# Attention block: the products with v in two groups of five pairs per unit, and TensorE's attention work in strict source order

## The chip, the cores and the metric

The kernel runs on one core of a Trainium2 chip. A core has a TensorE for matrix products (PE; PEld is its weight load), a VectorE (DVE), a ScalarE (ACT), a GpSimd (POOL) and a SyncE that issues DMAs (SP). The metric is the device time of one execution in microseconds (us). The kernel before takes 1155.64 us, the median of three runs from 1153.95 to 1157.52.

## What is computed

Attention with a learned position bias, over 4 batches, 8 heads, 576 positions and 64 dimensions a head, followed by two feed-forward layers on 2304 tokens of 512 features. All is float32.

```python
scores = scale * np.matmul(q, k.transpose(0, 1, 3, 2)) + bias      # bias: a small network of the positions
scores = scores - np.max(scores, axis=-1, keepdims=True)
attn = np.exp(scores)
attn = attn / (np.sum(attn, axis=-1, keepdims=True) + 1e-09)
x = np.matmul(attn, v)                                             # -> 2304 x 512
h = x @ w_in;  x = (h * np.clip(h + 3.0, 0.0, 6.0) / 6.0) @ w_out
out = (1 / (1 + np.exp(-(x @ w_gate))) * (x @ w_val)) @ w_out2
```

## The kernel before

The program has four stages: the position bias (to about 57 us of the profile), attention (to about 337 us), and the two feed-forward layers. The change touches attention alone.

Attention works in 16 units, each two heads of one batch, and each unit in nine steps. Steps 0 to 7 take 128 queries of one head, the two heads in turn; step 8 takes the last 64 queries of both heads. A step t goes through these functions:

- `scores` (line 365): four matmuls of 128x288, ten of them in step 8, into a PSUM tile "s" (two buffers, two banks each). Then VectorE adds the bias into an SBUF tile "u" and keeps the row's minimum (line 378).
- `expo` (line 392): ScalarE's exponential into the tile "p" or "pm", with the row's sum.
- `trans` (line 426): four transposes of 128x128 on TensorE into a PSUM tile "tr" (three buffers, one bank each), which VectorE or ScalarE copies out to the tile "ptm" (`evac`, the letters of `PT_EVAC`).
- `trans_rem` (line 440): after steps 1, 3, 5 and 8, one transpose (two after step 8) for the last 64 keys of both heads, into another "tr" tile and from there to the tile "ptr", on ScalarE.
- `invert` (line 397) and `turn_inv` (line 407): twice a unit, after steps 5 and 8, VectorE inverts the sums, ScalarE spreads them, and three or two transposes into a "tr" tile turn them; copies of VectorE and ScalarE bring them to the tile "inv".
- `av` (line 450): the products with v, in two groups a unit, one for each half of the queries (a = 0, 1), into the PSUM tile "av" (one buffer). A group has five pairs (g = 0 to 4), each pair one product for each head, written to the two halves of the partitions; the first four read ptm, the last reads ptr. A float32 product shows as two matmul records, so a pair shows as four. `av_out` (line 464) multiplies by inv on VectorE into the input of the next layer.

`slot_of_two` (line 490) takes two steps at a time. Slot i traces, in this order: the scores of steps 2i and 2i+1, the products that `AV` holds for the slot, the two exponentials, `invert` for the steps of the slot before, `turn_inv` for the steps of two slots before, `trans` and `trans_rem` for the steps of the slot before, and a cast of the next unit's queries and keys. Some slots also carry a piece of preparing the first layer's weights, on ScalarE, VectorE and GpSimd. `AV` (lines 479 to 485) puts three pairs of a group in one slot and two in the next, so that eight slots in nine hold products.

A planner (the framework's scheduler) puts the instructions into each engine's queue. It takes the source order as a priority, and lets an instruction pass an earlier one of the same engine where it reckons the earlier one is not ready. Each engine then executes its queue in order. `tc.issue_after(x)` binds everything traced inside it, on the engine of x, to come behind x in that queue; it adds no wait. The kernel before binds the transposes of a slot behind the last score matmul traced (line 516) and nothing else of TensorE.

Of the kernel before, what the change touches and what calls it, by code (L numbers as in the profile page):

```python
# [1 line left out]

# [1 line left out]

# [14 lines left out]
P = 128  # L19
B, H, S, D = 4, 8, 576, 64  # L20
# [4 lines left out]
HS = S // 2  # L25
# [71 lines left out]
def block_kernel(ctx: ExitStack, tc: tile.TileContext, q, k, v, mlp, w_in, w_out, w_gate, w_val, w_out2, dist_d,  # L97
                 rows_d, out):
    nc = tc.nc
# [199 lines left out]
    Pm = [apool.tile([P, S], F32, name=f"pm{i}") for i in range(2)]  # L299
    ident = apool.tile([P, P], F32, name="ident")  # L300
    stat = apool.tile([P, 5, NSTEP, 2], F32, name="stat")
    low, sums = [stat[:, i, :, 0] for i in range(2)], [stat[:, i, :, 0] for i in range(2, 5)]
    spread = apool.tile([P, 5 * P], F32, name="spread")
# [10 lines left out]
    def load_v(n):  # L314
        vn[n] = a2.tile([P, 10, D], F32, name="vn")
        return nc.sync.dma_start(vn[n], v[n])

    def load_bias(p, c):
        n = min(P, S - P * c)
        rows_of = nbias[c][15 : 15 + n * (8 * RK - 1)].rearrange("(i q) -> i q", i=n)  # L320
        for h in range(2):
            o = bias_t[c][:, h] if c < 4 else bias_m[64 * h : 64 * h + 64]
            i = rows_of[:, RK * (2 * p + h) : RK * (2 * p + h) + S]
            if c == 4 and h == 1:
                nc.sync.dma_start(o[:, 0:512], i[:, 64:S])
                nc.sync.dma_start(o[:, 512:S], i[:, 0:64])
            else:
                nc.sync.dma_start(o, i)
# [23 lines left out]
    NS = NU * NSTEP  # L352
    ptm = apool.tile([P, 2, 4, S], F32, name="ptm")
    ptr = apool.tile([P, S], F32, name="ptr")
    pts, us, avs, last_u, last_s = {}, {}, {}, [None], [None]

    seq = [(n, s) for n in range(NU) for s in range(NSTEP)]

    def keys(s, h, a):

        if s < 8 or h == 0:
            return [(HS * a, 0, HS)]
        return [(64, 0, HS)] if a == 0 else [(64 + HS, 0, HS - 64), (0, HS - 64, 64)]

    def scores(t):
        n, s = seq[t]
        Q, K = Qs[n % 2], Ks[n % 2]
        ps = pp.tile([P, 2, 512], F32, name="s")
        todo = [(s % 2, s // 2)] if s < 8 else [(0, 4), (1, 4)]
        for a in range(2):  # L370
            mm = [(h, c, r, part) for h, c in todo for r in range(2) for part in keys(s, h, a)]
            for i, (h, c, r, (k0, o, w)) in enumerate(mm):
                q0 = (0, S + P)[h] + P * c if c < 4 else (512, S)[h]
                last_s[0] = nc.tensor.matmul(ps[:, a, o : o + w], Q[:, q0 : q0 + P], K[:, r, h, k0 : k0 + w],  # L374
                                             start=(i == 0), stop=(i == len(mm) - 1))
        u = a2.tile([P, S], F32, name="u", bufs=3)
        bt = bias_t[s // 2][:, s % 2] if s < 8 else bias_m
        last_u[0] = nc.vector.tensor_tensor_reduce(  # L378
            out=halves(u), in0=ps[:, :, 0:HS], in1=halves(bt), op0=ALU.add, op1=ALU.min, scale=-0.125, scalar=3e38,
            accum_out=low[n % 2][:, s : s + 1])  # L380
        us[t] = u
# [25 lines left out]
    def turn_inv(n, c0, c1):  # L407

        ps = pp.tile([P, 4, P], F32, name="tr", bufs=3)
        for c in range(c0, c1):  # L410
            nc.tensor.transpose(ps[:, c % 3], spread[:, P * c : P * c + P], ident)  # L411
        if c1 == 3:
            evac("A", inv[:, 0 : 3 * P].rearrange("p (c q) -> p c q", c=3), ps[:, 0:3])
        else:
            evac("V", inv[:, 3 * P : 4 * P], ps[:, 0])
            for h in range(2):
                r = slice(64 * h, 64 * h + 64)
                evac("VA"[h], inv[r, 4 * P : S], ps[r, 1, r])

    def evac(eng, dst, src):  # L420
        if eng == "A":
            nc.scalar.copy(dst, src)  # L422
        else:
            nc.vector.tensor_copy(dst, src)  # L424

    def trans(t):
        n, s = seq[t]
        if s < 8:
            ps = pp.tile([P, 4, P], F32, name="tr", bufs=3)
            c, h = divmod(s, 2)  # L430
            for kc in range(4):
                nc.tensor.transpose(ps[:, kc], pts[n, c][:, h, 64 * h + P * kc : 64 * h + P * kc + P], ident)  # L432
            evac(PT_EVAC[s], ptm[:, h, :, P * c : P * c + P], ps)
        else:
            ps = pp.tile([P, 4, P], F32, name="tr", bufs=3)
            for kc in range(4):
                nc.tensor.transpose(ps[:, kc], Pm[n % 2][:, P * kc : P * kc + P], ident)
            evac("VA"[n % 2], ptm[:, :, :, 512:S], ps.rearrange("p c (h q) -> p h c q", h=2))

    def trans_rem(n, c):  # L440

        ps = pp.tile([P, 4, P], F32, name="tr", bufs=3)
        nc.tensor.transpose(ps[:, 0], pts[n, c].rearrange("p h s -> p (h s)")[:, 512 : 512 + P], ident)
        if c == 3:
            nc.tensor.transpose(ps[0:64, 1], Pm[n % 2][:, 512:S], ident)
            for h in range(2):
                evac("AV"[h], ptr[64 * h : 64 * h + 64, 512:S], ps[0:64, 1, 64 * h : 64 * h + 64])
        evac("A", ptr[:, P * c : P * c + P], ps[:, 0])

    def av(n, a, g):  # L450
        if g == 0:
            avs[a] = pp.tile([P, 512], F32, name="av", bufs=1)
        ps = avs[a]
        vt = vn[n]
        cols = slice(HS * a, HS * a + HS)
        if g < 4:
            for h in range(2):
                nc.tensor.matmul(ps[64 * h : 64 * h + 64, 0:HS], vt[:, 4 * h + g], ptm[:, h, g, cols],  # L458
                                 start=(g == 0), stop=False)
        else:  # L460
            for h in range(2):
                nc.tensor.matmul(ps[64 * h : 64 * h + 64, 0:HS], vt[:, 8 + h], ptr[:, cols], start=False, stop=True)  # L462

    def av_out(n, a):
        p, b = divmod(n, B)
        i = S * b + HS * a
        while i < S * b + HS * a + HS:
            j, o = divmod(i, 2 * TW)
            w = min(2 * TW - o, S * b + HS * a + HS - i)
            k = i - S * b - HS * a  # L470
            nc.vector.tensor_tensor(out=xj[j][:, p, o : o + w], in0=avs[a][:, k : k + w],
                                    in1=inv[:, HS * a + k : HS * a + k + w], op=ALU.mult)
            i += w

    REM = {1: 0, 3: 1, 5: 2, 8: 3}
# [3 lines left out]
    AV = {}  # L479
    for n in range(NU):  # L480
        i = (NSTEP * n + 5) // 2 + 2
        j = max(i + 2, (NSTEP * n + 8) // 2 + 2)
        for a, first in ((0, i), (1, j)):
            AV[first] = [(n, a, g) for g in range(3)]
            AV[first + 1] = [(n, a, g) for g in range(3, 5)]

    def steps(i):
        return [t for t in (2 * i, 2 * i + 1) if 0 <= t < NS]

    def slot_of_two(i):  # L490

        for t in steps(i):
            scores(t)
            n, s = seq[t]
            p, b = divmod(n, B)
            if s == 0:
                last_v[0] = load_v(n)
            if b == B - 1 and p + 1 < NPAIR and (s % 2 == 1 or s == 8):
                load_bias(p + 1, s // 2)
        for n, a, g in AV.get(i, ()):  # L500
            av(n, a, g)
            if g == 4:
                av_out(n, a)
        for t in steps(i):
            expo(t)
        for t in steps(i - 1):
            n, s = seq[t]
            if s in (5, 8):
                invert(n, s // 6 * 3, s // 6 * 2 + 3)
        for t in steps(i - 2):  # L510
            n, s = seq[t]
            if s in (5, 8):
                turn_inv(n, s // 6 * 3, s // 6 * 2 + 3)
        for t in steps(i - 1):
            n, s = seq[t]
            with tc.issue_after(last_s[0].ins):
                trans(t)
                if s in REM:
                    trans_rem(n, REM[s])
        for t in steps(i):  # L520
            if t in PREP:
                n, h = PREP[t]
                prep(n, h)
            for k, (n, h) in PREP.items():
                if h == 1 and n + 1 < NU and t == k + 3:
                    load_qk(n + 1)
# [6 lines left out]
    with ExitStack():  # L533
# [15 lines left out]
        ps = bp.tile([P, 2, 512], F32, name="s")[:, 0]  # L549
# [39 lines left out]
        for G in range(NG):  # L589
# [9 lines left out]
            ps = bp.tile([P, 2, 512], F32, name="s")  # L599
            for d0, d1 in ((0, min(nd, 512)), (512, nd)):  # L600
                for ct in range(4):
                    if d0 < d1:
                        nc.tensor.matmul(line(ps)[32 * ct : 32 * ct + 32, d0:d1], w2bd, hid[ct][:, d0:d1],
                                         start=True, stop=True)
# [44 lines left out]
        for i in range(NSLOT):  # L649
            slot_of_two(i)  # L650
            if i == NS // 2:
                w = keep.tile([P, 8 * TW], F32R, name="early")
# [119 lines left out]
        for part2, t in todo:  # L772
            for f in range(NH * part2, NH * part2 + NH):
# [3 lines left out]
                g = begun.pop(f) if f in begun and t == 0 else None  # L777
                if g is None:
                    g = hardswish(fp.tile([P, TW], F32, name="g", bufs=2), project(t, slots[2 * f % NALL]))
# [113 lines left out]
        for v, (p, j) in enumerate(visits):  # L893
# [9 lines left out]
            for n in range(2):  # L903
                t = 2 * j + n
# [48 lines left out]
```

## Time and profile before

| | |
|---|---|
| median of the runs | 1155.64 us (1153.95 to 1157.52) |
| the profiled execution | 1153.65 us, of which 1151.9 is the span from the first to the last instruction |
| busy in the span | PE 1129.9 us (98%), DVE 770.0 (67%), ACT 589.0 (51%), POOL 426.2 (37%) |
| granted clock of TensorE | 1.00, the higher level (2.4 GHz), in the whole span |
| largest groups of attention on PE | scores 111.5 us (672 matmuls), first four pairs 79.1 (512), transposes of p 74.0 (512) |

A row of the timeline merges neighbours that have the same line and form: start, duration, engine, line, operation, tiles, shape and count, and in brackets the idle time before it with what ended it. Matmuls are pipelined, so rows of PE overlap, and the distance between two starts is what a row took of TensorE's time. In the chain of waits each piece is the time until the next piece begins, so there the pieces add up.

### The profile page before, as it was taken

To read this page: it belongs to the slowest core of one execution; us is meant where nothing else is said; L and a number is where in the kernel's file an instruction comes from. 1 tells how busy PE (TensorE), PEld (TensorE's weight loads), DVE (VectorE), ACT (ScalarE), POOL (GpSimd) and SP (SyncE) were. 2 spreads that over 40 slices of the span, in tenths; PEclk is the share of its full clock that TensorE was granted. 3 is DMA by queue.
4 is the path that set the end of the run, shared out by engine and by line. 5 is a ranking of instruction groups with operands and counts; after the bars stand their busy time and mean duration, and the time that the engine had idled before them with its cause. 6 is when DMAs were issued, how large, how long until landed. Compare 5 with 4: busy or idle time off the path is not lost.

```text
span 1151.9 us, 19179 instructions
## 1 busy us (share of the span) xinstructions
PE 1129.9 (98%) x6878; PEld 1008.9 (88%) x6878; DVE 770.0 (67%) x1487; ACT 589.0 (51%) x1288; POOL 426.2 (37%) x340
## 2 busy tenths in 40 slices
PE   8799999999999999999999999999999999999998
PEld 3287777777789999999999999989899899998997
DVE  8987888897768888365376775585367656643443
ACT  7988888887765544454455454342333232221221
POOL 0154645554225432331347444261333223311311
PEclk9999999999999999999999999999999999999999
DMA  6854546364013665259467659976878848757532
GB/s 206 298 163 121 158 130 177 113 201 116 14 42 110 206 237 187 116 181 340 150 227 276 244 193 366 388 264 251 303 254 311 312 167 316 275 190 247 192 110 74
DMA packets 83503, 236.82 MB, mean 206 GB/s; under 512 B 9936, under 2 KB 12624, under 8 KB 83408
## 3 DMA queue, kind: packets, MB, share of 16 engines
q1 hardware_dynamic: 83408, 235.60, 59.4%
q8 instruction: 54, 0.88, 0.3%
q14 instruction: 41, 0.34, 0.1%
HBM read 154.15 MB, written 81.41 MB: 205 GB/s over the span
## 4 chain that ended last, share of the span: by engine, by line
PE 85%; DVE 5%; ACT 3%; issue 2%; POOL 1%; DMA 1%; DVEq 0%; ACTq 0%; POOLq 0%; SPq 0%
PE o L700 17%; PE h L834 11%; PE o L834 11%; PE o L889 6%; PE h L889 6%; PE h L637 5%; PE h L635 5%; PE h L636 5%; PE s L374 5%; PE av L458 5%; PE tr L432 4%; PE av L462 1%; DVE u L378 1%; PE tr L411 1%; ACT p L394 1%
## 5 line engine op out<-in xcount | busy, mean ns | idle before, releaser
L700 PE MATMUL o<-gh,slot 128*128 128x384 f32 x768 | 195.1, 334 | 1.8 <-DVE take L424 1.8
L700 PEld LDWEIGHTS o<-gh,slot 128*128 128x128 f32 x768 | 138.5, 188 | 2.4 <-DVE take L424 2.1
L700 PE MATMUL o<-gl,slot 128*128 128x384 f32 x384 | 128.5, 335 | 0.7 <-DVE gl L686 0.7
L378 DVE CUSTOM_DVE_ANT_0 u<-s,bias 128x576 f32<-128x576 f32 x128 | 93.7, 754 | 30.3 <-PE s L374 26.8
L374 PE MATMUL s<-k,q 128*128 128x288 f32 (+2 forms) x672 | 111.5, 304 | 1.3 <-DVE stat L378 0.9
L394 ACT ACTIVATE p<-u,stat 128x576 f32<-128x576 f32 x128 | 98.9, 775 | 23.8 <-DVE stat L378 23.3
L870 POOL TENSOR_TENSOR gp<-s,gp 128x384 fp32r<-128x384 f32 x36 | 39.4, 1108 | 176.1 <-ACT gp L869 91.3
L685 ACT CAST gh<-g 128x384 fp32r<-128x384 f32 x94 | 48.5, 516 | 97.3 <-DVE g L642 97.0
L642 DVE SCALAR_TENSOR_TENSOR g<-g,h 128x384 f32<-128x384 f32 x94 | 51.6, 549 | 69.2 <-ACT g L641 69.2
L686 DVE TENSOR_TENSOR gl<-g,gh 128x384 fp32r<-128x384 f32 x94 | 63.3, 673 | 48.2 <-ACT gh L685 47.0
L374 PEld LDWEIGHTS s<-k,q 128*128 128x128 f32 x672 | 92.0, 189 | 2.8 <-issue 1.2
L207 POOL TENSOR_TENSOR hl<-corners,hl 128x512 fp32r<-128x512 f32 x42 | 57.1, 1366 | 94.1 <-ACT hl L206 79.1
L340 POOL TENSOR_TENSOR k<-early,one 128x576 fp32r<-128x576 f32 x30 | 35.0, 1170 | 138.8 <-PE s L374 62.7
L641 ACT ACTIVATE g<-h,half 128x384 f32<-128x384 f32 x94 | 54.5, 580 | 53.1 <-PE h L637 52.6
L458 PE MATMUL av<-ptm,vn 128*64 128x288 f32 x512 | 79.1, 419 | 0.2
L834 PE MATMUL o<-x,slot 128*128 128x384 f32 x432 | 78.2, 336 | 0.0
L834 PE MATMUL h<-x,slot 128*128 128x384 f32 x432 | 77.8, 335 | 0.0
L834 PEld LDWEIGHTS h<-x,slot 128*128 128x128 f32 x432 | 75.2, 188 | 0.7
L834 PEld LDWEIGHTS o<-x,slot 128*128 128x128 f32 x432 | 75.1, 188 | 0.4 <-DVE sum L424 0.3
L432 PE MATMUL tr<-ident,p 128*128 128x128 f32 x512 | 74.0, 277 | 0.4 <-ACT ptr L422 0.2
L700 PEld LDWEIGHTS o<-gl,slot 128*128 128x128 f32 x384 | 72.0, 188 | 1.4 <-DVE gl L686 1.4
L870 POOL TENSOR_TENSOR x<-s,x 128x384 fp32r<-128x384 f32 x36 | 40.9, 1149 | 82.3 <-ACT x L869 48.6
(154 smaller groups left out, 2709.5 us busy)
## 6 DMA issues: line engine op xcount, KB each, us to landing
w<-hl SPq DMA_DIRECT2D x67, 512.0 KB, 3.3
slot<-w SPq DMA_DIRECT2D x67, 512.0 KB, 5.7
raw<-in_part_dram SPq DMA_DIRECT2D x50, 512.0 KB, 4.1
x<-xc SPq DMA_DIRECT2D x56, 384.0 KB, 6.3
sum<-sum SPq DMA_DIRECT2D x72, 256.0 KB, 3.7
early<-xc SPq DMA_DIRECT2D x28, 384.0 KB, 6.0
nbias<-ptm SPq DMA_DIRECT2D x36, 295.5 KB, 3.1
early<-in_part_dram SPq DMA_DIRECT2D x32, 288.0 KB, 4.5
```

The lines of the kernel that those rows point to most:

```text
L374: last_s[0] = nc.tensor.matmul(ps[:, a, o : o + w], Q[:, q0 : q0 + P], K[:, r, h, k0 : k0 + w], start=(i == 0), stop=(i == len(mm) - 1))
L378: last_u[0] = nc.vector.tensor_tensor_reduce(out=halves(u), in0=ps[:, :, 0:HS], in1=halves(bt), op0=ALU.add, op1=ALU.min, scale=-0.125, sc ...
L394: nc.scalar.activation(probs(t), us.pop(t), AF.Exp, bias=low[n % 2][:, s : s + 1], scale=-1.0, accum_out=sums[n % 3][:, s : s + 1])
L432: nc.tensor.transpose(ps[:, kc], pts[n, c][:, h, 64 * h + P * kc : 64 * h + P * kc + P], ident)
L458: nc.tensor.matmul(ps[64 * h : 64 * h + 64, 0:HS], vt[:, 4 * h + g], ptm[:, h, g, cols], start=(g == 0), stop=False)
L635: nc.tensor.matmul(ps[:, 0:TW], wh, XH[:, c], start=(c == 0), stop=False)
L636: nc.tensor.matmul(ps[:, 0:TW], wl, XH[:, c], start=False, stop=False)
L686: last_g[0] = nc.vector.tensor_tensor(out=gl, in0=g, in1=gh.bitcast(F32), op=ALU.subtract)
L700: nc.tensor.matmul(os[c][:, 0:TW], sl[:, r, P * c : P * c + P], x, start=(first and r == 0 and x is gh), stop=(last and x is gl))
L834: nc.tensor.matmul(ps[b], sl[:, r, o : o + P], x[:, c, s], start=(k < 4 and i == 0), stop=(i == len(mm) - 1), skip_group_check=True)
L870: nc.gpsimd.tensor_tensor(out=G[:, i, 1], in0=s, in1=G[:, i, 0].bitcast(F32), op=ALU.subtract)
L889: nc.tensor.matmul(os[i], x[:, P * i : P * i + P], slots[(base + 14 + e) % NALL][:, r], start=first, stop=last)
```

## The change

The products of a group, which stood as three pairs in one slot and two pairs in the next, now stand as five pairs in the later of the two slots. And each score matmul, transpose and product with v of attention is bound behind the one traced just before it, so that TensorE's queue has them in the order of the source. The older binding of the transposes is dropped with that. No instruction is added or removed; the two projections that the next layer begins at the end of attention are not bound.

```diff
-    pts, us, avs, last_u, last_s = {}, {}, {}, [None], [None]
+    pts, us, avs, last_u, last_pe = {}, {}, {}, [None], []
+
+    @contextmanager
+    def in_turn():
+        with ExitStack() as order:
+            if last_pe:
+                order.enter_context(tc.issue_after(last_pe[-1].ins))
+            yield last_pe.append
...
-                last_s[0] = nc.tensor.matmul(ps[:, a, o : o + w], Q[:, q0 : q0 + P], K[:, r, h, k0 : k0 + w],
-                                             start=(i == 0), stop=(i == len(mm) - 1))
+                with in_turn() as done:
+                    done(nc.tensor.matmul(ps[:, a, o : o + w], Q[:, q0 : q0 + P], K[:, r, h, k0 : k0 + w],
+                                          start=(i == 0), stop=(i == len(mm) - 1)))
...
         for a, first in ((0, i), (1, j)):
-            AV[first] = [(n, a, g) for g in range(3)]
-            AV[first + 1] = [(n, a, g) for g in range(3, 5)]
+            AV[first + 1] = [(n, a, g) for g in range(5)]
...
             n, s = seq[t]
-            with tc.issue_after(last_s[0].ins):
-                trans(t)
-                if s in REM:
-                    trans_rem(n, REM[s])
+            trans(t)
+            if s in REM:
+                trans_rem(n, REM[s])
```

The matmuls and transposes of `turn_inv`, `trans`, `trans_rem` and `av` are wrapped in `in_turn` in the same way as those of `scores`.

## Rows read from the trace of the kernel before

**Rows 1.** Stage, length, busy PE PEld DVE ACT POOL, clock, DMA: attention; units 7-8.

```profile
66.48:336.60 270.12, 267.19 (x2006) 204.38 (x2005) 212.70 (x543) 217.13 (x557) 127.44 (x95) 1.00 0.41 118
168.93:203.18 34.25, 34.15 (x258) 26.13 (x258) 27.92 (x72) 28.77 (x74) 18.56 (x15) 1.00 0.61 181
```

**Rows 2.** The chain of waits, 150 to 172 us: start, us, what.

```profile
159.86 0.87 PE tr L432 x8
...
161.89 1.61 PE av L458 x12
163.50 1.02 PE tr L432 x8
...
164.63 1.05 PE s L374 x8
165.69 0.64 PE av L458 x4
166.32 0.48 PE av L462 x4
...
167.94 1.77 PE s L374 x14
```

**Rows 3.** TensorE's timeline: a wait of scores, and a long burst of products.

```profile
152.78 0.77 PE L374 MATMUL s<-k,q 128*128 128x288 f32 x4 [0.21 <-DVE stat L378]
...
187.35 2.47 PE L458 MATMUL av<-ptm,vn 128*64 128x288 f32 x12
```

**Rows 4.** TensorE's timeline in slot (a), from 178.69, and slot (b), from 189.75.

```profile
178.69 0.44 PE L411 MATMUL tr<-ident,spread 128*128 128x128 f32 x2
...
179.43 0.90 PE L374 MATMUL s<-k,q 128*128 128x288 f32 x5
180.24 0.66 PE L432 MATMUL tr<-ident,p 128*128 128x128 f32 x4
...
189.75 0.55 PE L411 MATMUL tr<-ident,spread 128*128 128x128 f32 x3
...
190.93 0.91 PE L374 MATMUL s<-k,q 128*128 128x288 f32 x5
191.68 0.27 PE L443 MATMUL tr<-ident,p 128*128 128x128 f32 x1
...
192.38 0.71 PE L458 MATMUL av<-ptm,vn 128*64 128x288 f32 x4
```

**Rows 5.** TensorE's timeline: a remainder's transpose that waited.

```profile
299.71 0.33 PE L443 MATMUL tr<-ident,p 128*128 128x128 f32 x1 [0.71 <-ACT inv L422]
```

**Rows 6.** VectorE's timeline in slots (a) and (b).

```profile
177.04 0.75 DVE L378 CUSTOM_DVE_ANT_0 u<-s,bias 128x576 f32<-128x576 f32 x1
...
177.71 0.75 DVE L378 CUSTOM_DVE_ANT_0 u<-s,bias 128x576 f32<-128x576 f32 x1
...
179.19 0.41 DVE L424 COPY inv<-tr 128x128 f32<-128x128 f32 x2
...
191.74 0.76 DVE L378 CUSTOM_DVE_ANT_0 u<-s,bias 128x576 f32<-128x576 f32 x1 [2.84 <-PE s L374]
...
192.59 0.76 DVE L378 CUSTOM_DVE_ANT_0 u<-s,bias 128x576 f32<-128x576 f32 x1
```

**Rows 7.** ScalarE's timeline in slot (b).

```profile
188.16 0.73 ACT L336 CAST q<-early 64x640 fp32r<-64x640 f32 x1
188.79 0.78 ACT L394 ACTIVATE p<-u,stat 128x576 f32<-128x576 f32 x1
...
189.56 0.78 ACT L394 ACTIVATE p<-u,stat 128x576 f32<-128x576 f32 x1
...
190.32 0.49 ACT L405 COPY spread<-stat 128x128 f32<-128x128 f32 x2
190.71 0.48 ACT L422 COPY inv<-tr 128x384 f32<-128x384 f32 x1
...
192.54 0.78 ACT L394 ACTIVATE p<-u,stat 128x576 f32<-128x576 f32 x1 [0.24 <-DVE stat L378]
```

More of the change, by code (lines that the diff above doesn't have):

```diff
@@ L1 @@
-from contextlib import ExitStack
+from contextlib import ExitStack, contextmanager
 import numpy as np
@@ L410, in turn_inv @@
         for c in range(c0, c1):
-            nc.tensor.transpose(ps[:, c % 3], spread[:, P * c : P * c + P], ident)
+            with in_turn() as done:
+                done(nc.tensor.transpose(ps[:, c % 3], spread[:, P * c : P * c + P], ident))
         if c1 == 3:
@@ L431, in trans @@
             for kc in range(4):
-                nc.tensor.transpose(ps[:, kc], pts[n, c][:, h, 64 * h + P * kc : 64 * h + P * kc + P], ident)
+                with in_turn() as done:
+                    done(nc.tensor.transpose(ps[:, kc], pts[n, c][:, h, 64 * h + P * kc : 64 * h + P * kc + P], ident))
             evac(PT_EVAC[s], ptm[:, h, :, P * c : P * c + P], ps)
@@ L436, in trans @@
             for kc in range(4):
-                nc.tensor.transpose(ps[:, kc], Pm[n % 2][:, P * kc : P * kc + P], ident)
+                with in_turn() as done:
+                    done(nc.tensor.transpose(ps[:, kc], Pm[n % 2][:, P * kc : P * kc + P], ident))
             evac("VA"[n % 2], ptm[:, :, :, 512:S], ps.rearrange("p c (h q) -> p h c q", h=2))
@@ L442, in trans_rem @@
         ps = pp.tile([P, 4, P], F32, name="tr", bufs=3)
-        nc.tensor.transpose(ps[:, 0], pts[n, c].rearrange("p h s -> p (h s)")[:, 512 : 512 + P], ident)
+        with in_turn() as done:
+            done(nc.tensor.transpose(ps[:, 0], pts[n, c].rearrange("p h s -> p (h s)")[:, 512 : 512 + P], ident))
         if c == 3:
-            nc.tensor.transpose(ps[0:64, 1], Pm[n % 2][:, 512:S], ident)
+            with in_turn() as done:
+                done(nc.tensor.transpose(ps[0:64, 1], Pm[n % 2][:, 512:S], ident))
             for h in range(2):
@@ L457, in av @@
             for h in range(2):
-                nc.tensor.matmul(ps[64 * h : 64 * h + 64, 0:HS], vt[:, 4 * h + g], ptm[:, h, g, cols],
-                                 start=(g == 0), stop=False)
+                with in_turn() as done:
+                    done(nc.tensor.matmul(ps[64 * h : 64 * h + 64, 0:HS], vt[:, 4 * h + g], ptm[:, h, g, cols],
+                                          start=(g == 0), stop=False))
         else:
             for h in range(2):
-                nc.tensor.matmul(ps[64 * h : 64 * h + 64, 0:HS], vt[:, 8 + h], ptr[:, cols], start=False, stop=True)
+                with in_turn() as done:
+                    done(nc.tensor.matmul(ps[64 * h : 64 * h + 64, 0:HS], vt[:, 8 + h], ptr[:, cols], start=False,
+                                          stop=True))
     def av_out(n, a):
```

## The prediction, made before the changed kernel was run

> **What bounds the kernel now.** I read the table of busy time by stage first. Between the second unit's first score and the end of attention TensorE is busy for 267.2 of 270.1 us, at a granted clock of 1.00, while VectorE is busy for 212.7 and ScalarE for 217.1 of them [rows 1]. So attention is TensorE's, with VectorE and ScalarE at about 80%. The order of work repeats every two units (nine slots); one such stretch, units 7 and 8, takes 34.25 us [rows 1], and I price this stretch. A busy TensorE is not TensorE at its peak, so next I read the chain of waits, where each piece counts from one release to the next [rows 2]. Three pairs of products with v take 1.61 us, two pairs 0.64 + 0.48 = 1.12. The difference, 0.49, is one pair; each burst has 0.15 besides. Eight transposes behind a burst take 1.02 us, and 0.87 behind other transposes: another 0.15. So entering and leaving the products costs 0.30 us a burst, whatever its length. Transposes cost 0.109 each (0.87/8), an ordinary score step 0.53 (1.05 for two); the row of 14 is one ordinary step and the long one of step 8, so that is 1.24.
>
> The pure TensorE work of two units is then: 16 score steps x 0.53 and 2 x 1.24, 10.9; 92 transposes (46 a unit by the loops: 36 for the eight two-head steps and the shared one, 5 of remainders, 5 of sums) x 0.109, 10.0; 20 pairs x 0.485, 9.7; 8 bursts x 0.30, 2.4. Together 33.0 of 34.25, so about 1.3 us is waiting. Two places of it are to be seen: a three-pair burst that starts at 187.35 and has its next transposes only 2.40 us later [rows 3, 4], where a plain one takes 1.61, and scores held back 0.21 us by VectorE behind a slot with no products [rows 3].
>
> **The change, part by part.** *Merging.* 64 bursts become 32. No matmul is removed. That takes 4 x 0.30 = 1.2 us from each two units and 32 x 0.30 = 9.6 us from the kernel. All of it lies on TensorE, which sets the end of the stage.
>
> The Trainium skill (TensorEngine Tiling, Key Properties) says that a change of tiling mode drains TensorE; the trace agrees [rows 2], 0.30 us in and out of the 128x64 products. By that rule alone the kernel would end 9.6 us sooner; rival A is that outcome.
>
> *The first three pairs one slot later.* They no longer ask for evictions made just before; the long burst becomes a plain one. What else hangs on them is covered: the eviction of the products stays in its slot; the next unit overwrites ptm and ptr only after transposes that stand behind the whole group in the same slot; the accumulator has a whole slot between its two groups; the v tile is freed where it was. If this cover failed, an eviction would wait for at most a burst, 2.6 us, twice a unit. No DMA moves, and nothing passes a queue of SP or POOL.
>
> *Strict order.* The ordering itself is no instruction. But it takes away what TensorE did while a transposed tile had no free PSUM buffer. There are three "tr" buffers. Let T be the four transposes of trans, r the remainder's of trans_rem, I those of turn_inv. Now, in the slot of the second inversion (a), the order is I (two transposes), T, r, then four score matmuls and one more, and only then the second T [rows 4]. In the slot of step 8 (b), it is I (three), T, T, then five score matmuls of the next slot, and then r [rows 4]. In both, the fourth "tr" tile of a slot is put off until a buffer is free. In strict order TensorE waits for it, and the next slot's scores, then VectorE and ScalarE, wait behind it. Where r could not be put off far enough, the trace shows such a wait: 0.71 us for ScalarE's eviction of the inversion [rows 5].
>
> Such slots also become bare. Now eight slots in nine hold products; then only four do, and both (a) and (b) fall in slots without. A burst is when the others catch up: VectorE sat idle 2.84 us, most of it under one [rows 6].
>
> I price both from the slot's first score (time 0). Scores end at 0.53 and 1.06. An element-wise step u starts 0.2 after TensorE has gone on from its scores [rows 4, 6] and the next 0.67 after it [rows 6]: 0.74 and 1.41, free at 2.08. An exponential starts 0.80 after its u, and the next 0.77 after it [rows 6, 7]: 1.54, 2.31, free at 3.08.
> (a) I ends at 1.28, T at 1.72, r at 1.83; then the second T wants I's buffer. Its two VectorE copies (0.41 together, [rows 6]) come behind the second u: 2.5. Its one ScalarE copy, 0.2, comes before the exponentials or behind them, 3.3. The wait is 0.7 to 1.5; I take 1.0, since weight preparation also sits in VectorE's queue.
> (b) I ends at 1.39, T and T at 2.26; r wants I's buffer. Its eviction (0.48) comes on ScalarE behind both exponentials and two spread copies (0.39 to the next), as in the trace [rows 7]: 3.08 + 0.39 + 0.48 = 3.95, a wait of 1.7, and 2.4 if a cast of the queries (0.73, in the same queue, [rows 7]) falls in between. If ScalarE's queue has it behind the first exponential alone, 2.8: a wait of 0.5. I take 1.9, near the order that stands in the rows.
> (c) The slot after (b) also has four "tr" tiles, but behind a burst, with the other two engines idle; the rest have three, one per buffer, and want them after two score steps. The trace shows 0.2 us of waiting after such a slot [rows 3]. From 0 to 0.7 for two units, the upper end being [rows 5] once; I take 0.3.
> The order of VectorE's and ScalarE's queues in the changed kernel is what I can't read from this trace; the bounds above are those of their possible orders.
>
> The sum for two units: -1.2 for the bursts, -1.3 for the old waits, +1.0 + 1.9 + 0.3 = +3.2 for new ones: +0.7 us, and over eight such stretches +5.6. The profiled execution took 1153.65 us (span 1151.9), 2.0 below the median of 1155.64; the same difference on the median gives 1161. What follows attention is untouched and starts so much later.
>
> The Trainium skill (TensorEngine Tiling, PSUM Bottleneck) warns that tiling speeds up TensorE but not the eviction of PSUM. Here the trace agrees [rows 3]: behind a slot with no products the scores already wait for VectorE.
>
> **The rivals.**
> A, faster: evictions come free in time. Its place is ScalarE's and VectorE's queues in (a) and (b). If the evictions of I stand ahead of the second exponential, the waits are at their lower ends, 0.7 + 0.5 + 0 = 1.2: -1.2 - 1.3 + 1.2 = -1.3, x 8 = -10 us: 1145. It decides from new waits under 2.1 us in two units. For it: a TensorE that is busy throughout and a sure 9.6 us. Against: ScalarE takes both exponentials ahead of that eviction [rows 7].
> B, no difference: new waits equal what is gained, 2.5 us in two units: 1156. For it: the likeliest terms above miss this by only 0.7.
> C, clearly slower: the waits run into each other. (a) at 1.5, (b) at 2.4, (c) at 0.7 make 4.6: +2.1 x 8 = +17, 1172. Two bare slots follow each other once in nine, and (b) stands in the second; VectorE and ScalarE enter it late. Against it: a five-pair burst follows at once, under which they catch up.
> D, the groups don't merge and no order changes: 1156. The order is on every matmul of attention, so I give it little.
>
> **How the numbers follow.** A measurement of this kernel can't tell less than 0.3%, 3.5 us, from no change. Forecast 0.45 (0.38 of it slower, 0.07 within 0.3%); A 0.27, faster; B 0.13 (0.10 within, 0.03 faster); C 0.13, slower; D 0.02, within. So faster 0.30, same 0.19, slower 0.51. The range reaches from A's 1145 to C's 1172, with half of each left outside: 0.2 in all.
>
> **What would show it.** The products with v should stand in 32 rows of 20 matmuls, each about 2.6 us to the next transpose; with 64 rows D holds. The stretch of two units should be near 34.9 us; A wants 33, C 36. TensorE's waits should be two for each two units, on the second T of (a) and the r of (b), released by the inversion's evictions, of 1.0 and 1.9 us. I am wrong on the price if the waits sit there but are short, wrong on the place if they sit on scores waiting for u, and wrong on the gain if a 20-matmul row with its exit takes longer than five pairs and 0.30.

## The result, and the profile after

The changed kernel takes 1161.59 us (1159.18 to 1162.96), the kernel before beside it 1153.95: a ratio of 1.0059, with a 95% interval of 1.0041 to 1.0077. So it is slower by about 7 us, under 1% but clear of the noise. The 1153.95 is the median of six runs, the three that give the 1155.64 above and three more. The profiled execution took 1159.18 us, of which 1157.4 is the span.

The table by stage comes first, as in [rows 1]: stage, length, busy PE, PEld, DVE, ACT, POOL, granted clock, DMA share, GB/s; attention from the second unit's first score, and units 7 and 8.

```profile
65.83:342.43 276.60, 258.09 (x2005) 206.43 (x2004) 204.05 (x543) 213.96 (x557) 127.78 (x95) 0.99 0.39 115
170.40:205.26 34.86, 32.58 (x258) 26.25 (x258) 26.88 (x72) 28.49 (x73) 18.65 (x15) 1.00 0.59 179
```

TensorE is now busy for 258.1 of 276.6 us, where it was 267.2 of 270.1: 9.1 us of its busy time are gone, and 18.5 us of idle time stand where there were 2.9. Units 7 and 8 take 34.86 us, against 34.25 before. What follows attention is as long as it was (814.9 us from 342.5 to the end; 815.3 from 336.6 before).

The chain of waits (start, us, what) shows a group of products and what surrounds the one long wait, which is the answer to [rows 2].

```profile
173.44 2.09 PE av L473 x16
175.53 0.48 PE av L478 x4
...
176.64 0.69 DVE ptm L434
...
177.61 0.25 DVE ptm L434
...
178.22 0.75 DVE u L387
...
179.01 1.02 ACT p L403 x3
...
180.66 0.22 ACT inv L432
...
180.92 0.66 PE tr L443 x4
```

A group is one row of 16 and one of 4, 2.57 us together, which is five pairs at 0.485 and 0.15. The attention part of the trace holds 32 such groups, none broken; 31 of them take 2.58 us to the next transpose and one 3.71, at a lower clock (last section). And where the chain of before stayed on TensorE in the rows shown, it now leaves TensorE: copies and a bias step on VectorE, the exponentials and the copy of the inverses on ScalarE, and only then the second T of slot (a).

TensorE's timeline gives the three waits of these two units, in the slots of [rows 4] and the one after (b).

```profile
177.01 1.32 PE L383 MATMUL s<-k,q 128*128 128x288 f32 x8
...
178.82 0.27 PE L456 MATMUL tr<-ident,p 128*128 128x128 f32 x1
180.92 0.66 PE L443 MATMUL tr<-ident,p 128*128 128x128 f32 x4 [1.83 <-ACT inv L432]
...
191.67 0.33 PE L456 MATMUL tr<-ident,p 128*128 128x128 f32 x1 [0.30 <-ACT inv L432]
...
197.14 0.33 PE L456 MATMUL tr<-ident,p 128*128 128x128 f32 x1 [0.15 <-ACT inv L432]
```

The bracket counts only idle time. From start to start, against the 0.109 us that a transpose takes otherwise, (a) costs 1.99 us, (b) 0.46, (c) 0.32: 2.77 together, all three released by a copy of the inverses on ScalarE. The page's list of the costliest groups has the idle time of the whole kernel: the T's stood 13.7 us in all, 12.8 of them for that copy.

```profile
L443 PE MATMUL tr<-ident,p 128*128 128x128 f32 x512 | 72.9, 276 | 13.7 <-ACT inv L432 12.8
```

Why the copy is late in (a) stands in the timelines of the two other engines. VectorE first (answering [rows 6]):

```profile
178.22 0.75 DVE L387 CUSTOM_DVE_ANT_0 u<-s,bias 128x576 f32<-128x576 f32 x1
...
179.57 0.41 DVE L434 COPY inv<-tr 128x128 f32<-128x128 f32 x2
```

And ScalarE, in (a) and then in (b) (answering [rows 7]):

```profile
179.01 0.78 ACT L403 ACTIVATE p<-u,stat 128x576 f32<-128x576 f32 x1 [1.13 <-DVE stat L387]
...
179.79 0.76 ACT L403 ACTIVATE p<-u,stat 128x576 f32<-128x576 f32 x1
...
180.66 0.21 ACT L432 COPY inv<-tr 64x64 f32<-64x64 f32 x1
...
191.16 0.46 ACT L432 COPY inv<-tr 128x384 f32<-128x384 f32 x1
191.51 0.78 ACT L403 ACTIVATE p<-u,stat 128x576 f32<-128x576 f32 x1
```

In (a), VectorE was still copying the transposed weights of the slot before (ptm and ptr in the chain) when the scores were ready, so u began at 178.22, 1.21 us after the slot's first score; ScalarE itself stood idle for 1.13 us and then did both exponentials ahead of a copy of 64x64 that takes 0.21. VectorE's own two copies of the inverses were done by 179.98, 0.9 us sooner. In (b) the copy stands ahead of both exponentials, unlike in [rows 7].

### The profile page after: what moved, and what is told of

The parts are those of the page before. It is cut to its first block, busy times and chain, and to the rows that moved or that the text cites. A ratio compares the mean times of both kernels' runs of the same rounds, so it can differ in the third digit from the quotient of the medians.

```text
span 1157.4 us, 19219 instructions
## 1 busy us (share of the span) xinstructions
PE 1119.9 (97%) x6878; PEld 1011.0 (87%) x6878; DVE 761.2 (66%) x1487; ACT 585.4 (51%) x1288; POOL 427.0 (37%) x340
## 4 chain that ended last, share of the span: by engine, by line
PE 81%; ACT 7%; DVE 4%; issue 2%; DMA 1%; POOL 1%; SPq 0%; ACTq 0%; DVEq 0%; POOLq 0%
PE o L715 17%; PE h L849 11%; PE o L849 10%; PE o L904 6%; PE h L904 6%; PE h L651 5%; PE h L652 5%; PE h L650 5%; PE av L473 4%; PE s L383 4%; PE tr L443 3%; ACT p L403 3%; DVE u L387 1%; DVE ptm L434 1%; PE av L478 1%
## 5 line engine op out<-in xcount | busy, mean ns | idle before, releaser
L403 ACT ACTIVATE p<-u,stat 128x576 f32<-128x576 f32 x128 | 98.9, 774 | 35.4 <-DVE stat L387 34.2
L383 PE MATMUL s<-k,q 128*128 128x288 f32 (+2 forms) x672 | 105.7, 302 | 1.0 <-DVE stat L387 0.6
L443 PE MATMUL tr<-ident,p 128*128 128x128 f32 x512 | 72.9, 276 | 13.7 <-ACT inv L432 12.8
L443 PEld LDWEIGHTS tr<-ident,p 128*128 128x128 f32 x512 | 57.4, 141 | 23.1 <-ACT inv L432 14.4
L207 POOL TENSOR_TENSOR slot<-z,slot 128x512 fp32r<-128x512 f32 x19 | 28.5, 1503 | 116.0 <-ACT slot L206 116.0
L885 POOL TENSOR_TENSOR x<-s,x 128x384 fp32r<-128x384 f32 x36 | 40.8, 1145 | 82.0 <-ACT x L884 48.3
```

The source lines that it names most:

```text
L207: eng.tensor_tensor(out=slot[:, 1], in0=z, in1=slot[:, 0].bitcast(F32), op=ALU.subtract)
L383: done(nc.tensor.matmul(ps[:, a, o : o + w], Q[:, q0 : q0 + P], K[:, r, h, k0 : k0 + w], start=(i == 0), stop=(i == len(mm) - 1)))
L403: nc.scalar.activation(probs(t), us.pop(t), AF.Exp, bias=low[n % 2][:, s : s + 1], scale=-1.0, accum_out=sums[n % 3][:, s : s + 1])
L443: done(nc.tensor.transpose(ps[:, kc], pts[n, c][:, h, 64 * h + P * kc : 64 * h + P * kc + P], ident))
L885: nc.gpsimd.tensor_tensor(out=G[:, i, 1], in0=s, in1=G[:, i, 0].bitcast(F32), op=ALU.subtract)
```

## The experiments

The theory: merging saves 0.30 us a burst, as reckoned, and the strict order takes back more than that, since in a slot with four "tr" tiles TensorE stands for an eviction that ScalarE does behind its exponentials. The rivals were that a merged group gains nothing, that the slots without products are bound by VectorE and ScalarE whatever the tiles, and that the copy's place alone decides. Ratios below are to the kernel before, run beside, with 95% intervals; before took 1154.35 to 1156.24 us there.

**One half of the change alone.** First the merged groups without the order:

```diff
-            AV[first] = [(n, a, g) for g in range(3)]
-            AV[first + 1] = [(n, a, g) for g in range(3, 5)]
+            AV[first + 1] = [(n, a, g) for g in range(5)]
```

> The kernel before with the merged groups alone: five pairs in the later slot, but the transposes bound behind the last score matmul as before, and nothing else bound. In its queue the products stand in 51 bursts, not 32, since single pairs are split off. Theory (the waits of strict order for a free tr buffer eat the gain): with the fourth tr tile of a slot put off again, the waits of 2.0 and 0.46 us that the changed kernel shows in two units mostly vanish, and 13 bursts x 0.30 = 3.9 us are kept: 1147 to 1155, below the kernel before or at it. Rival (the loss comes from the merging itself, since the slots that are left without products starve TensorE): as slow as the changed kernel, 1159 to 1163.

1155.74 us, 1.002 (1.0008 to 1.0032): no gain, just above the theory's range and below the rival's. The trace has 55 bursts, not 32: left free, the planner breaks groups up. TensorE's timeline:

```profile
109.20 0.70 PE L458 MATMUL av<-ptm,vn 128*64 128x288 f32 x2
...
111.77 1.68 PE L458 MATMUL av<-ptm,vn 128*64 128x288 f32 x12
```

So merging needs some order to be a merging at all, and this run doesn't test merged groups by themselves. Then the order without the merged groups:

```diff
-            AV[first + 1] = [(n, a, g) for g in range(5)]
+            AV[first] = [(n, a, g) for g in range(3)]
+            AV[first + 1] = [(n, a, g) for g in range(3, 5)]
```

> The changed kernel with its groups split again into three pairs and two in consecutive slots: strict order alone, 64 bursts. Theory (strict order costs where a slot has no products ahead of its fourth tr tile): nearly every slot has a burst again under which the inversion's copies are made, so the two waits shrink to under 0.5 us in two units, and the time is that of the kernel before or a little less, 1148 to 1156. Rival (strict order costs by itself, wherever four tr tiles stand in a slot): the waits of about 2.5 us in two units stay and the 9.6 us of the merged bursts are lost, 1165 to 1171.

1165.19 us, 1.0102 (1.0087 to 1.0117), as the rival had it: the strict order costs by itself, with products in eight slots of nine. TensorE's timeline, the second T of slot (a) and the r of the slot behind (b):

```profile
184.52 0.66 PE L443 MATMUL tr<-ident,p 128*128 128x128 f32 x4 [0.57 <-ACT ptm L432]
...
200.62 0.33 PE L456 MATMUL tr<-ident,p 128*128 128x128 f32 x1 [0.28 <-ACT inv L432]
```

All waits make 2.4 us in two units. Those for a fourth tile are 1.4 of it, half of the changed kernel's 2.77; the rest stands on a score step and in a stretched burst, as in [rows 3]. The second T of (a) waits 0.73 us, while it waits 1.99 in the changed kernel, whose slot (a) has no products. So merging on top of the order brings 1.0102 - 1.0059, some 5 us (2 to 8 by the intervals), and not 9.6: the rest goes into longer waits in the slots that it empties.

**The order at the groups alone.** Everything stays before or behind a group, the transposes behind the slot's scores as in the kernel before, but between two groups scores of the next slot may pass a transpose (`av` uses `burst`, `trans` and `trans_rem` use `behind_s`):

```diff
-    def in_turn():
+    def in_turn(burst=False, behind_s=False):
         with ExitStack() as order:
-            if last_pe:
-                order.enter_context(tc.issue_after(last_pe[-1].ins))
-            yield last_pe.append
+            for x in (since if burst else []) + last_av[-1:] + (last_s if behind_s else []):
+                order.enter_context(tc.issue_after(x.ins))
+            if burst:
+                since.clear()
+            yield (last_av if burst else since).append
```

> The changed kernel with strict order at the bursts alone: everything traced before a group of products comes before it in TensorE's queue, everything traced after it comes after, and between two groups the planner may again put a transpose behind later scores. The queue has 32 whole bursts, and the fourth tr tile of slots (a) and (b) stands behind the next slot's score matmuls, as in the kernel before. Theory (merging pays 1.2 us in two units and the strict order between transposes and scores takes more than that back): two units take 33.0 to 33.8 us, the kernel 1146 to 1152. Rival (merged groups leave slots bare, and that costs as much as they bring, whatever the order): 1154 to 1158, as the kernel with merged groups and no strict order.

1154.67 us, 1.0001 (0.9991 to 1.0012), with 32 whole groups. Steady pairs of units take 33.55 us, as the theory had it (33.0 to 33.8), 1.3 less than in the changed kernel. The total is the rival's, level with before: some pairs are longer, one of 36.68. TensorE's timeline shows both kinds:

```profile
176.54 1.47 PE L385 MATMUL s<-k,q 128*128 128x288 f32 x8
178.44 0.66 PE L446 MATMUL tr<-ident,p 128*128 128x128 f32 x4 [0.43 <-ACT inv L435]
...
255.02 0.78 PE L385 MATMUL s<-k,q 128*128 128x288 f32 x4 [1.68 <-DVE stat L390]
...
259.69 0.33 PE L459 MATMUL tr<-ident,p 128*128 128x128 f32 x1 [1.64 <-ACT inv L435]
```

With eight score matmuls passed ahead of it, the second T of (a) waits 0.58 us from start to start instead of 1.99. That shows that the wait is one of order: the same work, the same groups, another sequence. The two long waits of the irregular pair come from VectorE, where its timeline has two steps that take far longer than the 0.69 and 0.32 us of the same steps elsewhere, one of weight preparation ahead of u and one of the inversion ahead of the spread copy. GpSimd's timeline, the last two rows, has steps beside both (last section):

```profile
252.67 1.52 DVE L188 SCALAR_TENSOR_TENSOR z<-raw,z 128x512 int32<-128x512 int32 x1
...
256.75 1.25 DVE L412 TENSOR_SCALAR stat<-stat 128x3 f32<-128x3 f32 x1
...
252.24 2.96 POOL L340 TENSOR_TENSOR k<-early,one 128x576 fp32r<-128x576 f32 x2
255.16 2.81 POOL L344 TENSOR_TENSOR k<-early,k 128x576 fp32r<-128x576 f32 x2
```

**That order, and the copy of the inverses on VectorE.** On top of the edit before:

```diff
             for h in range(2):
                 r = slice(64 * h, 64 * h + 64)
-                evac("VA"[h], inv[r, 4 * P : S], ps[r, 1, r])
+                evac("V", inv[r, 4 * P : S], ps[r, 1, r])
```

> The changed kernel, with the strict order kept only around the groups of products (transposes may be passed by scores between two groups) and the 64x64 copy of the inverses on VectorE. Theory: the wait of 0.58 us that ScalarE's copy left on the second T goes to 0.3 or less, since VectorE's copies are done sooner: 0.3 x 8 = 2 to 3 us less than with the order at the groups alone, 1151 to 1153 us. Rival (VectorE gets later by one more copy and holds back scores, or another eviction is last): 1154 to 1157 us, the wait standing on another row.

1150.77 us, 0.9953 (0.9938 to 0.9967): the only version that does the whole work and is faster than both kernels beyond the noise, and just below the theory's 1151 to 1153. In TensorE's timeline the T in the place of the waiting one has no wait left, and the group follows at once:

```profile
208.72 1.47 PE L385 MATMUL s<-k,q 128*128 128x288 f32 x8
210.06 0.63 PE L446 MATMUL tr<-ident,p 128*128 128x128 f32 x4
210.61 2.16 PE L476 MATMUL av<-ptm,vn 128*64 128x288 f32 x16
```

Steady pairs of units take 33.03 us, others up to 35.2. To see whether it is the copy alone that gains, the same one line was changed in the kernel before:

> The kernel before with one edit, the 64x64 copy of the inverses on VectorE instead of ScalarE: 64 bursts, no order. It asks whether the gain of the run with the order at the groups and this copy on VectorE (0.9953 of before) needs the merged groups at all. Theory (it does): before has few waits behind this copy, so it moves by less than 2 us, 1153 to 1157 us beside 1155. Rival (the copy's engine alone is worth it, in any order): 1148 to 1151 us.

1153.87 us, 0.9996 (0.9987 to 1.0005): nothing. So the 0.43% between this and the run above, about 5 us, are what the merged groups, with the order that keeps them whole, are worth once the evictions are in time.

**Without the fourth tile.** The transposes of the inverted sums and their copies are left out, with one memset in their place, in the changed kernel and in the one before. No slot has four "tr" tiles then:

```diff
+    nc.vector.memset(inv, 1.0)
...
-        for t in steps(i - 2):
-            n, s = seq[t]
-            if s in (5, 8):
-                turn_inv(n, s // 6 * 3, s // 6 * 2 + 3)
```

> The changed kernel without the transposes of the inverted sums and their copies (the scaling by the sums is left out: the tile of inverses is set to one, once). No slot is left with a fourth tr tile. Theory (the strict order costs only by fourth tr tiles): the waits of 1.99, 0.46 and 0.32 us in two units vanish, and so do ten transposes of 0.109 = 1.09: two units fall from 34.86 to 31.0 (up to 31.6 if other small waits appear), attention ends about 29 us sooner, and the kernel takes 1130 to 1136 us. Rival (slots without products are bound by VectorE and ScalarE, whatever the tiles): waits of 1 to 2 us stay on transposes of weights or on scores in the slots without products, two units take 32.5 to 33.5, and the kernel 1141 to 1150.

> The kernel before with the same part left out (scaling by the sums; the tile of inverses is set to one, once). Theory: there the free order had already hidden most of what the fourth tr tiles cost, so little more than the ten transposes goes: two units from 34.25 to 32.5 to 33.2, the kernel 1140 to 1147 us. So without fourth tr tiles the changed kernel would be 8 to 13 us below this one: the whole gain of 32 bursts fewer, 9.6 us, would show. Rival (slots without products are bound by the other two engines): the two kernels without turns end within 3 us of each other.

The changed kernel falls to 1137.46 us (0.9839, 0.9819 to 0.9858), by 24 us; the kernel before to 1144.59 (0.9901, 0.9886 to 0.9915), by 11.7. What is left out is the same in both. So the fourth tile costs the strict order some 12 us more than it costs the free one, and without it the change is a gain of 7.1 us, where with it it is a loss. That speaks against empty slots as the bound. But the theory had the changed kernel at 1130 to 1136 and a difference of 8 to 13: of the six pairs of units behind the first, two take 31.17 and 31.29 us, as expected, and the others 32.0 to 34.2, with waits of this kind, in TensorE's timeline:

```profile
181.27 0.66 PE L450 MATMUL tr<-ident,pm 128*128 128x128 f32 x4 [0.39 <-ACT ptm L433]
...
245.25 0.76 PE L384 MATMUL s<-k,q 128*128 128x288 f32 x4 [0.84 <-DVE stat L388]
```

Those are for the weights' evictions and for VectorE, the rival's kind: a smaller part of the cost is the emptied slots' own. In the pair of 34.23 us the chain of waits also holds 7.86 us of a DMA that ScalarE's weight preparation needs.

**Moving the eviction, with the strict order kept.** Four tries. First the 64x64 copy on VectorE, the one-line diff above on the changed kernel:

> The changed kernel with one copy of 64x64 elements (the second half of the last sums) moved from ScalarE to VectorE. In the changed kernel the wait of 2.0 us before the second transposes of slot (a) ends with this copy, which stands behind two exponentials on ScalarE. Theory: the buffer is free when VectorE has made its third copy, some 0.7 us sooner; 8 x 0.7 = 5 to 6 us less than the changed kernel, 1154 to 1157. Rival (the transposes wait there for something else, such as their own exponentials, and the copy only ends last by chance): within 2 us of the changed kernel, 1159 to 1163.

1157.79 us, 1.0026 (1.001 to 1.0042): 3.8 us of the 6.8 come back, just short of the theory's range and of the rival's. Slot (a) waits 1.43 us instead of 1.99 and now ends with VectorE's copy of the inverses, as the theory had it, and (b) changes between 1.36 and 0.47 from pair to pair. Next the inverses' transposes right ahead of their group of products, one or two slots later:

```diff
         for n, a, g in AV.get(i, ()):
+            if g == 0:
+                turn_inv(n, 3 * a, 2 * a + 3)
             av(n, a, g)
...
-        for t in steps(i - 2):
-            n, s = seq[t]
-            if s in (5, 8):
-                turn_inv(n, s // 6 * 3, s // 6 * 2 + 3)
```

> The changed kernel with the transposes of the inverted sums moved: not two slots behind their step, but right ahead of the group of products whose result they scale, so that their copies are made while the products run. Theory: a slot without products then has three tr tiles, the inversion's buffer is free long before the fourth tile of a slot with products, and the 2.8 us of waiting in two units fall below 0.6: two units take 32.1 to 32.8 us instead of 34.86 and the kernel 1140 to 1147. Rival (the slots without products are bound by VectorE and ScalarE anyway, so the wait moves to the exponentials or the scores): above 1153.

1158.82 us, 1.0039 (1.0017 to 1.006). The theory's 1140 to 1147 was wrong: the wait moved. Now the inverses' transposes ask for a buffer that a T still holds, TensorE's timeline:

```profile
192.95 0.55 PE L421 MATMUL tr<-ident,spread 128*128 128x128 f32 x3 [1.82 <-ACT ptm L432]
193.42 3.52 PE L473 MATMUL av<-ptm,vn 128*64 128x288 f32 x16
```

Then the inverses traced ahead of the exponentials (`turn_inv` of the slot moved above `expo`):

```diff
+        for t in steps(i - 2):
+            n, s = seq[t]
+            if s in (5, 8):
+                turn_inv(n, s // 6 * 3, s // 6 * 2 + 3)
         for t in steps(i):
             expo(t)
...
-        for t in steps(i - 2):
-            n, s = seq[t]
-            if s in (5, 8):
-                turn_inv(n, s // 6 * 3, s // 6 * 2 + 3)
```

> The changed kernel with one pair of source blocks exchanged: the transposes of the inverted sums and their copies are traced ahead of the slot's two exponentials. TensorE's order is the same to the last instruction; only the priority of the copies on ScalarE and VectorE rises. Theory (the wait is for ScalarE's copy behind the exponentials): in slot (a) the wait of 2.0 us falls to VectorE's 0.7 to 1.2, slot (b) stays at 0.2 to 0.5, and the kernel takes 1150 to 1156. Rival (the copy is late because ScalarE itself is late there, so that its place in the queue doesn't matter): 1159 to 1163.

1159.64 us, 1.004 (1.0025 to 1.0055), and it decides nothing: the planner left ScalarE's queue as it was, as its timeline in slot (a) shows, and the wait was 1.99 us again.

```profile
181.64 0.78 ACT L403 ACTIVATE p<-u,stat 128x576 f32<-128x576 f32 x1 [1.13 <-DVE stat L387]
...
183.29 0.21 ACT L432 COPY inv<-tr 64x64 f32<-64x64 f32 x1
```

Then the exponentials traced last in their slot:

```diff
-        for t in steps(i):
-            expo(t)
...
                 if h == 1 and n + 1 < NU and t == k + 3:
                     load_qk(n + 1)
+        for t in steps(i):
+            expo(t)
```

> The changed kernel with the two exponentials traced last in their slot, so that ScalarE and VectorE give every eviction of a transposed tile priority over them; TensorE's order is the same. Theory (TensorE waits for tr buffers and for nothing else): all waits for buffers fall below 1 us in two units and the kernel takes 1147 to 1154. Rival (the exponentials are as late as the evictions, so that transposes wait for their input where they now wait for a buffer): 1159 or more.

1159.76 us, 1.0036 (1.0021 to 1.0051): the rival's time, though not its mechanism. This time the queue changed, but (a) still waits for a buffer, 1.47 us, for a ptm copy; one (b) waits 2.1 behind a step of weight preparation that itself stood for its DMA, in ScalarE's timeline:

```profile
191.92 0.67 ACT L174 ACTIVATE z<-raw 128x512 f32<-128x512 f32 x1 [1.56 <-DMA raw<-in_part_dram]
192.49 0.47 ACT L432 COPY inv<-tr 128x384 f32<-128x384 f32 x1
```

Last, with the order at the groups alone, the inverses' transposes behind those of the weights:

```diff
-        for t in steps(i - 2):
-            n, s = seq[t]
-            if s in (5, 8):
-                turn_inv(n, s // 6 * 3, s // 6 * 2 + 3)
         for t in steps(i - 1):
             n, s = seq[t]
             trans(t)
             if s in REM:
                 trans_rem(n, REM[s])
+        for t in steps(i - 2):
+            n, s = seq[t]
+            if s in (5, 8):
+                turn_inv(n, s // 6 * 3, s // 6 * 2 + 3)
```

> The changed kernel, with the strict order kept only around the groups of products and the transposes of the inverted sums behind those of the weights in their slot, so that the fourth tr tile asks for the buffer of a T, whose eviction is a wider copy, and not for that of the inverses. Theory (the wait is for the evictions of the inverses): the waits on T and r behind the inverses go, 1.0 to 1.3 us in two units, 1145 to 1150 us. Rival (four evictions in one slot are the cost, in any order): the wait stands on the inverses' transposes instead and is as long, 1153 to 1158 us.

1162.19 us, 1.0056 (1.004 to 1.0073), worse than either theory or rival had it. The fourth tile waits for a weight's copy behind the exponentials, with a preparation step ahead of these that here stood 1.68 us for its DMA, and now with the group of products right behind it, TensorE's timeline:

```profile
197.97 0.90 PE L424 MATMUL tr<-ident,spread 128*128 128x128 f32 x3 [2.96 <-ACT ptm L435]
198.80 3.24 PE L476 MATMUL av<-ptm,vn 128*64 128x288 f32 x16
```

Together these say: it is not the copy of the inverses as such, but any fourth tile in a slot whose eviction comes behind the slot's exponentials. Tracing it elsewhere moved the wait; letting TensorE do scores meanwhile, or taking the copy to the engine that is free sooner, shortened it. None of the four tries in strict order came down to the kernel before.

## Why the prediction came out right

It said 1161 us, from 1145 to 1172, and slower as the likeliest side. The mechanism holds: a saving on the bursts, eaten by waits for a fourth tile. That the number fits within 1 us is in part luck, since three pairs of errors cancelled. By its steps:

- *The price of a burst, 0.30 us, and 32 rows of 20 matmuls at about 2.6 us.* Right: 2.57. The busy time of TensorE in attention fell by 9.1 us against 9.6 reckoned, a rough check, since stretched bursts count as busy. The Trainium skill's rule in TensorEngine Tiling (Key Properties), that changing the tiling mode drains TensorE, agrees with that price a burst. The 9.6 us did not come off the kernel's time, but the pair of kernels without the fourth tile shows 7.1 of it.
- *The stretch of two units near 34.9 us.* Right: 34.86, with a first cancelling: the new waits came to 0.4 us less than put, and the rest of the stretch, 32.1, to 0.3 more than the 31.8 that the sum leaves for it. Over the whole stage it is less even than a constant 0.7 a pair: against before, the pairs counted from the first unit are longer by 1.1, 1.0, 0.6, 0.6 and 0.6, then shorter by 1.0, longer by 1.1, and the last two units by 2.4, 6.4 in all.
- *The old waits, 1.3 us, gone.* Right as far as the rows go: besides the three new ones no wait over 0.1 us stands in units 7 and 8.
- *The new waits: place, releaser and sum.* Right: the second T of (a), r of (b), and r of the slot behind, all released by ScalarE's copies of the inverses, 2.77 us against 3.2. The third had been named for the slot, without its row.
- *Their sizes.* Wrong for two of three, and the errors cancelled, the second time. (a) was put at 1.0, at most 1.5, and measured 1.99; (b) was put at 1.9 and measured 0.46, just under its lower bound of 0.5; (c) 0.32 as put, 0.3. In (a) the 1.0 stood between the two orders of ScalarE's queue, and the later one came, behind both exponentials, which alone makes 1.5. What goes beyond that upper bound is the start of u: the text had 0.74 us after the slot's first score, from a slot in which VectorE was free; it came 0.47 later, because VectorE was still copying the weights of the slot before, transposed behind the merged group. So the copy behind both exponentials ended 3.9 us after the first score and not 3.3. In (b) the text took the queue of [rows 7], the copy behind both exponentials; the planner put it ahead of both, behind pm, a ptr copy and a preparation step. The text had named that queue as what it couldn't read. Where the order of [rows 7] does come back, in the (b) at 297.48, with a cast of the queries ahead of the exponentials, the wait is 2.37 us, the text's upper end. The chain of waits of the changed kernel has it, the spread copies and the copy of the inverses behind the exponentials:

```profile
295.71 0.95 ACT p L403 x3
296.67 0.39 ACT spread L414 x2
297.05 0.38 ACT inv L432
...
297.48 0.33 PE tr L456
...
297.92 1.52 PE s L383 x8
299.43 3.23 PE av L473 x16
```

- *Emptied slots.* The text held that slots without products let the waits grow. The runs agree: the T of (a) waits 0.73 us with products in its slot and 1.99 without. An empty slot alone doesn't make the long wait, though: one (a) of the changed kernel, at 249.55, waits 0.73 us without products, since there ScalarE made a ptm copy ahead of both exponentials and the T took that buffer. It lies in the one pair of units that is shorter than before. And the text told the strict order's cost and the empty slots' as one; the order alone, with 64 bursts, is 10.6 us slower than before, which the text had not priced.
- *Rival A, evictions in time, 1145.* Its point was new waits under 2.1 us in two units. With the order loosened and the copy on VectorE a steady pair of units keeps one of 0.46 and a longer pair 1.8 in all, and the kernel is faster, 1150.77. So evictions in time do turn the change into a gain, about half of the 10 us that the rival promised, but not in the strict order that was asked about.
- *Rivals B to D.* The change is clear of the noise, so B, level, is out; D is out by the 32 whole groups. C's 2.4 us in (b) came once, at 297.48, and not in each two units.
- *Total.* +5.6 us was put on the median of before, 1155.64. The profiled executions differ by 5.5, the medians by 7.6, and the median of before came down to 1153.95 with three more runs: 2.0 too little of change on 1.7 too much of base, the third cancelling.

What stays open is how much the irregular pairs of units cost (36.68 us in one run with the order at the groups, 34.23 in one without the fourth tile). The rows show what stands beside them: preparation steps of the next layer's weights in VectorE's and ScalarE's queues, some standing for a DMA, and VectorE steps stretched beside GpSimd's. No run took the preparation away.

## What to carry to other kernels

Before binding an order by hand, count the buffers that a stretch of it asks for: each tile more than there are buffers can become a wait for an eviction, and its length is read from the evicting engine's queue, not from the copy's own 0.2 us. Bind what has to be together, here the products of a group, and leave the rest free to fill the wait; test the merging and the order apart, since either alone can hide what the other does. A stretch of work on the bounding engine that looks like pure cost may be the time in which the other engines catch up, so taking it out of a slot has a price there.

## What the hardware showed beside it

*TensorE's clock.* After the longest wait of the changed kernel TensorE's granted clock fell. TensorE's timeline has that wait:

```profile
297.48 0.33 PE L456 MATMUL tr<-ident,p 128*128 128x128 f32 x1 [2.20 <-ACT inv L432]
```

The table by stretches (stretch, length, busy PE, PEld, DVE, ACT, POOL, granted clock, DMA share, GB/s) goes on from there, and its last row stands behind the T of the slot (a) before it:

```profile
297.50:299.50 2.00, 2.00 (x12) 1.72 (x14) 0.96 (x3) 0.99 (x3) 2.00 (x2) 0.70 0.00 0
299.50:301.50 2.00, 2.00 (x10) 1.01 (x12) 1.81 (x5) 1.65 (x5) 0.32 (x1) 0.50 0.00 0
301.50:303.50 2.00, 2.00 (x18) 1.06 (x15) 0.31 (x2) 1.78 (x6) 0.00 (x0) 0.95 0.00 0
...
284.82:286.80 1.98, 1.98 (x16) 1.72 (x18) 1.28 (x4) 0.73 (x2) 0.00 (x0) 1.00 0.67 152
```

TensorE was idle for 2.20 us before 297.48. Behind that the clock fell to 0.50, the lower of its two levels (1.2 GHz), and was back at 1.00 after 303.5; behind an idle time of 1.82 us that ended at 284.82 it stayed at 1.00. The eight scores took 1.52 us instead of 1.05 and the group's first 16 matmuls 3.23 instead of 2.09, so this wait cost 1.6 us more than itself. The bursts of 3.52 and 3.24 us in two of the experiments above (2.16 otherwise in this view) stand behind idle times of 1.82 and 2.96 us, at granted clocks of 0.60 and 0.66. So idle time of the same length has gone both ways here. None of it was in the prediction.

*VectorE beside GpSimd.* In the irregular pair of the run with the order at the groups, VectorE's step of 252.67 spans the end of a GpSimd step at 253.65 and ends 0.55 us behind it; the one of 256.75 ends 0.03 behind the end of another. The fourteen profiled executions agree. Of four kinds of VectorE step in attention (the sums' 128x6 and three 128x512 forms of the weights' preparation), 741 lie beside no GpSimd step, and none of these takes over 1.3 times its usual time; 71 do take longer, all beside a GpSimd step, and all end 0.03, 0.28 or 0.55 us, by kind, behind such a step's end. Another 73 overlap one and keep their time. So in these rows VectorE stood for GpSimd, though no run moved GpSimd's work to test it.
